# Blockwise-causal attention and an MLP mixer on one core: another order table for the whole run

## The chip, the core and the metric

The kernel runs on one core of a Trainium2 chip. The core has a matrix engine (TensorE: PE, with its weight loads shown apart as PEld), three engines that work on rows of data (VectorE: DVE, ScalarE: ACT, GpSimd: POOL) and a sync engine (SyncE: SP) that only issues transfers here. Each works through its own list of instructions in order, and waits on semaphores for the others. Transfers between HBM and the on-chip memory are issued by POOL, SP and ACT and carried out by 16 DMA engines.

The metric is the device time of one launch in microseconds (us). It is given as the median of several runs; one further execution, with the profiler on, gave the trace.

## The reference

Per batch (8) and head (8) a softmax attention over 576 positions with 64 columns a head, under a mask by blocks of 64; the heads are put side by side as `x` of 576 x 512. Then a mixer: across positions, then across columns, each with a residual.

```python
scores = scale * np.matmul(q, k.transpose(0, 1, 3, 2))     # q, k, v: [8, 8, 576, 64]
mask = (pos[:, None] // 64) >= (pos[None, :] // 64)
attn = softmax(np.where(mask, scores, -1e9))
x = np.matmul(attn, v).transpose(0, 2, 1, 3).reshape(8, 576, 512)
xt = x.transpose(0, 2, 1)
h = np.maximum(xt @ w_tok1, 0.0) @ w_tok2                  # 576 x 256, 256 x 576
u = x + h.transpose(0, 2, 1)
h2 = np.maximum(u @ w_ch1, 0.0) @ w_ch2                    # 512 x 1536, 1536 x 512
out = u + h2                                               # float32, [8, 576, 512]
```

## The kernel before

The kernel is written as a plan. Each piece of work is added by `P.add` with the engines that may do it, what it depends on and how many PSUM banks it takes: 1,492 operations in all, numbered in the order in which the code adds them. Nothing is issued while they are added. Then `P.placed()` walks a table of words, `ORDER` (lines 100 to 176), and issues the operations in its order:

```python
for word in ORDER.split():
    digits = word.rstrip("abcdefghstADPST")
    o, letters = self.ops[int(digits)], word[len(digits):]
    o.engine = self.ENGINE[letters[0]]
    ...
    for letter, (pools, note) in zip(letters[1:], o.take):
        note["pool"], note["slot"], note["home"] = pool_of[letter], self.SLOTS[letter][1], letter
```

The digits of a word are the operation's number. The first letter is its engine: T for TensorE, A for ScalarE, D for VectorE, P for GpSimd, S for SyncE. The letters behind it are the PSUM banks that it takes: a to d (`mm` in the profile), e to h (`late`), s and t (the two score banks of the opening, `sc`). The table therefore sets three things: the order of each engine's instructions, which of two engines does a piece where both may (evacuations of PSUM on ACT or DVE, the attention's tail copies on DVE or POOL, some stores on SP or ACT), and the banks. Waits follow from the data: an instruction waits for what wrote its operands, and for whoever read last what it overwrites.

The work of one batch passes these steps, with the lines that the profile names:

- Loads: q and k (`qk_sb`, L413 on POOL), transposed by DVE in blocks of 32 (L437); v in five pieces (`vals`, L463 on POOL). The weights come once: the token weights (L474), `w_ch1` in eight pieces of 192 KB (L497, `wc_sb`), `w_ch2` in three of 512 KB (L506, `wc_sb`).
- Scores: L562, four heads at a time, as tiles of 32 rows in four banks; ACT takes the exponentials into `e_sb` (L581 in the opening, L768 after it). A tail of 64 columns is copied into its own tile (L590) and its masked part cleared (L595), on DVE or POOL.
- Values: L612 and, for the last 64 positions, L665; DVE takes reciprocals (L632, L687) and scales into `x_sb` (L638, L693).
- Token mixing: L803, L807, then L836, L851 or L898, L929, L938; relus L789 (ACT) or L791 (DVE); DVE adds `u_sb` (L913). `u` is transposed by DMA on SP (L965, L975) or by TensorE (L985).
- Channel mixing up: L1026 plain, L1099 (`channel_up_half`) and L1226 (`channel_up_fast`) with products of sums and differences of blocks, for which `ws_sb` is made of the weights on DVE (L1057). Casts (L395 on ACT, L397 on DVE) and relus empty the banks.
- Channel mixing down: L1360, seven products of sums and differences of the relu's result (L1342) and of the weights, `wd_sb` (`weight_sums`, L1312, made by DVE once `w_ch2` is there). DVE folds the products with the residual into `o_sb` (L1406), which is stored (L1451; L1435 for the last 64 positions of all batches).

Where a product adds into a bank whose seed was written by another engine than TensorE, and which no matmul has opened, `cover` (L313) issues one more matmul into it first:

```python
def cover(bank):
    if P.bare(bank):
        nc.tensor.matmul(out=bank_of(bank), lhsT=ident, rhs=wc1_sb[:, 0, 0:512], start=True, stop=True)
```

`bare` looks at the pool that the table's bank letter stands for at that moment.

Of the kernel before, what the change touches and what calls it, by code (L numbers as in the profile page):

```python
# [27 lines left out]
class Plan:  # L28
# [72 lines left out]
    13S 16S 19S 22P 24P 5P 9D 2D 11D 8D 6D 3P 44Ta 12P 10P 4P 14D 30P 15D 17A 32P 1D 26P 18D 20A 28P 0A 45Tb 46Tc 47Td  # L101
    23D 25D 21D 7D 31D 174Tst 33D 175T 176A 177A 71Ta 61Tb 64Tc 182Ts 195A 196A 27D 81Td 183A 80Ta 201Tt 202A 60Tb 180Ts
    181A 29D 65Tc 197D 199Tt 76Td 178D 198D 36P 179D 200A 214Ts 215A 37P 35P 38P 34P 184Ta 188Tb 189T 190D 191D 207Tc
    208T 237Tt 238A 209D 210D 211Td 192Tb 216D 252P 254D 217D 193D 194D 220Ts 203Tc 204T 212D 213D 158P 205D 206D 185T
    155P 186D 221A 187D 218Tt 219A 233Ts 43P 156P 339Tb 239Tt 253D 340D 255P 257D 256D 234A 240A 42P 41P 39P 40P 337Td
    338A 222Tc 235D 236D 226Ta 227T 228D 223T 269Tbefg 271A 272A 249Th 224D 229D 225D 250D 251D 241Td 242T 243D 273A
    244D 157P 245Ta 246T 164P 247D 248D 348Tc 349T 350D 270A 281Tehfd 284A 230Tg 231D 282A 232D 343Ta 285A 261P 263D
    262D 258P 344D 276Tbcfg 277A 279A 159P 341Te 342A 280A 278A 283A 259D 260D 345Td 346T 347D 354Ta 355T 356D 313Tbfeg
    317A 316A 314A 315A 351Td 352T 353D 163P 387Tc 384Th 166P 301Taged 305A 390Tb 303A 302A 268P 165P 391T 274D 392D
    275D 388T 389D 304A 385T 306D 307D 308Tfdga 381Tb 264P 382T 408Te 409D 267P 312A 266P 265P 292Tc 295Ta 309A 318Tf  # L110
    386A 311A 296D 297D 289Th 290D 291D 160P 286Te 287D 288D 360Tg 366Ta 293D 310A 321Td 322D 323D 294D 319D 320D 400Th
    383A 416Tb 417A 161P 375Te 162P 376T 367T 368A 401A 421P 422D 423D 327Td 378Tc 372Tb 373T 374A 424P 328D 329D 404Tf
    405A 426D 377A 361T 427P 425D 428D 379T 380A 330Ta 362A 331D 332D 298Th 438Tdbfe 439A 430P 440A 324Ta 299D 432D 325D
    300D 369Tc 370T 326D 442A 429D 371D 450Tgdhb 441A 169P 363Ta 431D 364T 452A 333D 454A 451A 167P 357Te 358T 359A 365D
    393D 168P 482Tfcdb 485A 604P 484A 443P 453A 502Tg 436P 504Te 433P 503A 334D 335D 437P 435P 170D 486A 470Tadch 434P
    595P 505A 171D 444P 601P 483A 473A 445Tgbef 471A 172D 514Tc 448A 508Ta 472A 173D 515A 512Te 506Td 446A 509D 510Tc
    474A 513D 397Tgh 447A 475P 507D 449A 476P 394D 598P 477Tabef 398A 403Td 395D 480A 479A 511D 481A 493Te 396D 520Tb
    478A 490Tc 518Tf 521A 494D 407T 406D 519A 495D 597D 464Ta 596D 455Tb 461Tf 410D 458Te 399T 465D 491D 456D 457D 462D
    459D 466D 411T 463D 600D 402D 496Tb 522Ta 412D 516Tf 413T 523A 497D 599D 419S 517A 460D 762P 492D 499Tg 414D 759P
    467Ta 612Tdfec 498D 526D 415T 336D 615A 616A 614A 530Tcb 613A 487Te 500D 468D 469D 531Tf 533A 501D 617P 527D 545Tda  # L120
    532A 418D 618P 536T 611P 548A 524Tg 488D 489D 534Tf 537A 525D 610P 551T 528D 535A 624Thegc 605D 608P 552A 538T 606D
    628A 607P 540T 529D 627A 539D 678Td 626A 609P 603D 625A 549Tc 602D 679A 619Tgfeh 541D 550A 546Td 622A 760D 553T 623A
    763D 543T 620A 547D 676Te 621A 761D 544A 644Thgdf 542D 926P 677A 554D 555T 647A 764D 560Tbe 648A 556D 561Tc 929P
    563A 680Td 557D 765P 562A 684Tf 681D 645A 566T 558T 685D 646A 564Tc 567A 649D 559D 651Tdhgf 650P 565A 768P 638Tb
    653A 635Ta 772P 639D 568T 652A 640D 570T 636D 654A 637D 686Th 569D 655A 656Tbdga 571D 641Tf 660A 687D 629Tc 659A
    573T 642D 630D 689S 643D 632Ta 658A 631D 682Th 572D 657A 788Tgfdc 633D 634D 574A 673Tb 683D 790A 670Te 674D 789A
    664Ta 688S 675D 671D 579Tfh 672D 791A 665D 792A 666D 769D 783Tbgde 580A 667Tc 784A 661Ta 668D 581T 785A 669D 662D
    786A 663D 767D 787A 776Tbcgd 582D 842Ta 779A 766D 778A 575D 932P 840Te 780A 941P 770D 777A 583Tf 930D 773P 841A 576D
    843A 781P 820Tgcdb 939P 577D 585T 771P 821A 578D 824A 775P 584D 694Tae 850Tg 774P 690D 697A 587T 586D 822A 935P 691D
    823A 782P 692D 698Tb 851D 848Tc 588D 699A 700T 849D 695Tg 701A 704T 696D 702T 589T 705D 703D 693D 808Tdfca 931D 707T  # L130
    590D 810A 844Tg 812A 846Tb 845D 809A 793Tf 591T 708A 847D 811A 794D 795D 813P 815Tadge 592D 814P 805Tb 1024P 819A
    802Tc 594S 806D 818A 799Tf 807D 854S 803D 724Teh 817A 800D 709Tgb 801D 816A 727D 710Td 712A 725Tf 927D 711A 728Ta
    855S 928D 726A 715T 804D 796Td 729A 934D 730T 716A 713Tf 933D 731A 734T 420S 797D 798D 714A 732T 593S 735D 943Tcged
    733D 719T 945A 736D 717T 946A 720D 831Ta 944A 834Tg 718D 737T 947A 722T 835D 836D 738A 828Te 948P 832D 833D 950Tcfdg
    723A 829D 830D 837Th 721D 953A 852Ta 838D 952A 839D 857D 825Tb 951A 853D 876Tce 1036P 954A 877Td 858D 856S 879A 826D
    861Tfh 827D 1035P 878A 862Tg 859D 864D 891Tad 949P 863A 880Tb 940P 706D 894A 882T 739D 881A 942P 865Tg 897T 937D
    866A 938P 867T 936D 883A 884T 860D 1021P 868A 871T 885D 1030P 869T 898A 886T 872D 1027P 987Tcfba 870D 874T 887D
    1034P 990A 895Tg 988A 875D 889T 991A 1007Tb 740D 989A 896A 890D 955Tchaf 741D 892Te 959A 899T 1026D 956A 901T 893D
    958A 1009Tf 957A 1008D 902D 975Tcaeh 1010D 972Tb 978A 904T 900D 979A 960Tf 1025D 969Te 905A 743Tgh 961D 976A 973D
    1122P 974D 962D 977A 970D 971D 982Tdbcf 980D 744A 981D 1022D 966Ta 984A 963Te 1023D 745T 985A 967D 888D 1119P 986A  # L140
    964D 965D 983A 1037P 995Tb 968D 873A 998Tc 746D 1050Tfeda 1033P 996D 999D 992Tg 1000D 1054A 749T 993D 1053A 994D
    997D 1052A 1028D 1038Tcagd 1051A 1029D 1004Tb 1041A 1031D 1001Te 1125P 1040A 747Tf 1032D 1039A 1002D 1003D 1128P
    1005D 1006D 1082Tgace 1135P 748D 1017Tb 1084A 742D 751T 1083A 1018D 1086A 750D 1042A 1045Tageb 1085A 752D 1043P 753T
    1047A 1131P 1121D 757S 1049A 1120D 1044P 1048A 1077Tdcfg 754D 1064Tb 1080A 1124D 1061Te 755T 1046A 1065D 1062D 1063D
    1079A 1078A 1070Tfaec 1081A 756D 1067Td 1074A 1123D 1058Tg 1073A 1104Th 1066D 1059D 1071A 1060D 1130D 1072A 1055Tc
    1143Tbegf 1105A 1056D 1075P 1057D 1015Ta 1134P 1068D 1146A 1127D 1013Th 1145A 1069D 1102Tc 1129D 1147A 1076D 1144A
    1014D 1093Tg 1103A 1090Td 1016D 1136Tefbh 1126D 1020S 1099Tc 1137A 1094D 1114Ta 1091D 1092D 1140A 1100D 1087Te 1101D
    1139A 903D 1096Td 1088D 1112Th 1138A 1089D 758S 1108Tc 1095D 1115A 1141P 1113D 1106Tb 1132P 1175Tfeag 1097D 1142D
    1098D 1011Th 1133P 1107D 1179A 1336Td 1177A 1012D 1178A 1109D 1168Tgbeh 1176A 1110Ta 1116S 1171A 910Tcf 1170A 1111D
    1337A 1169A 1334Te 1117S 911D 906D 1148Tbadg 912T 907D 1150A 1019S 1172A 1151A 916T 1173P 913D 1152A 1174P 1149A  # L150
    908D 1118S 1180Tahdg 909D 1153Tc 1183A 914Tb 1154D 1184A 1155D 1181A 917D 1194Td 1182A 1335D 1159Tc 1191Tg 1195D
    1185Ta 1196D 1197Th 1160D 1192D 1165Te 1193D 920T 915D 1161D 1198D 1199D 1166D 1188Td 1167D 921D 1162Tg 1156Tc 1189D
    1249Teh 1190D 918T 1163D 1164D 1252A 1200D 1201D 922T 1186D 919D 1157D 1255T 1158D 924S 1279Tbd 1187D 923D 1280Tg
    1282A 1350Tc 1256A 1281A 1234Tea 1351A 1344Tf 1237A 1283Tc 1345D 1285T 1284A 1240T 1286A 1338Tg 1241A 1250Tf 1339D
    1253Tb 1251A 1287T 1202D 1254A 1348Te 1288D 1203D 1259T 1349A 1257T 1238Tc 1258D 1289T 1239A 1235Tg 1290D 1342Tf
    1236A 1244T 1291D 1343D 1356Te 1242T 1245D 1219Tbg 1243D 1360Tf 1260D 1220Tc 1361A 1357D 1262T 1222A 1292T 1364S
# [1404 lines left out]
```

## Time and profile before

| what | us |
|---|---|
| median of 3 runs | 287.9 |
| the three runs | 287.9, 285.44, 288.12 |
| the profiled execution | 286.21 |
| its span, first to last record | 284.4 |

The span is what the trace's times run over; the profiled execution's own time holds 1.8 us more, around it. The granted clock of TensorE was 0.997 of full speed in it. In the profile a line stands for engine, operation, output and input tile; "idle before" is the time that the engine stood still just before the group's instructions, with what ended that. TensorE's matmuls overlap one another, so the duration of one is longer than its distance to the next. Transfers are listed by the engine that issued them, with the time from issue to landing.

### The profile page before, as it was taken

To read this page: it belongs to the slowest core of one execution; us is meant where nothing else is said; L and a number is where in the kernel's file an instruction comes from. 1 tells how busy PE (TensorE), PEld (TensorE's weight loads), DVE (VectorE), ACT (ScalarE), POOL (GpSimd) and SP (SyncE) were. 2 spreads that over 40 slices of the span, in tenths; PEclk is the share of its full clock that TensorE was granted. 3 is DMA by queue.
4 is the path that set the end of the run, shared out by engine and by line. 5 is a ranking of instruction groups with operands and counts; after the bars stand their busy time and mean duration, and the time that the engine had idled before them with its cause. 6 is when DMAs were issued, how large, how long until landed. Compare 5 with 4: busy or idle time off the path is not lost.

```text
span 284.4 us, 9295 instructions
## 1 busy us (share of the span) xinstructions
PE 275.6 (97%) x3958; PEld 201.9 (71%) x3958; DVE 241.8 (85%) x520; ACT 178.3 (63%) x329; POOL 71.9 (25%) x123
## 2 busy tenths in 40 slices
PE   7799999999999999999999999999999999999994
PEld 2367565588776688986877658756789876568883
DVE  4678599999889898999998979859896997679983
ACT  3797969954998756887779866274533744651200
POOL 8977623701630451063232220000000000000000
PEclk9999999999999999999999999999999999999998
DMA  7999999955989792999699593201044501200157
GB/s 166 144 152 202 179 213 212 170 89 116 110 96 135 87 142 60 220 133 162 70 117 144 65 177 61 74 3 21 0 83 96 194 0 74 77 1 2 74 152 220
DMA packets 64890, 31.95 MB, mean 112 GB/s; under 512 B 53200, under 2 KB 55888, under 8 KB 64848
## 3 DMA queue, kind: packets, MB, share of 16 engines
q0 software_dynamic: 44896, 17.49, 53.9%
q1 hardware_dynamic: 19520, 13.21, 18.0%
q8 instruction: 31, 0.51, 0.7%
q10 hardware_dynamic: 432, 0.66, 0.7%
q14 instruction: 11, 0.09, 0.1%
HBM read 35.85 MB, written 9.44 MB: 159 GB/s over the span
## 4 chain that ended last, share of the span: by engine, by line
PE 78%; DMA 12%; DVE 4%; POOL 4%; issue 1%; POOLq 0%; DVEq 0%
PE late L1360 20%; DMA wc_sb<-in_moe_w_ch_dram 10%; PE mm L1360 9%; PE late L1226 8%; PE late L1099 7%; PE mm L1099 6%; PE mm L1226 5%; PE mm L562 4%; PE mm L612 3%; PE late L562 2%; PE late L898 2%; DMA qk_sb<-in_k_dram 2%; PE late L612 2%; PE mm L803 2%; PE late L803 2%; PE mm L898 1%
## 5 line engine op out<-in xcount | busy, mean ns | idle before, releaser
L768 ACT ACTIVATE e_sb<-late 128x512 bf16<-128x512 f32 x87 | 50.2, 612 | 15.0 <-PE late L562 6.6
L768 ACT ACTIVATE e_sb<-mm 128x512 bf16<-128x512 f32 x81 | 46.8, 611 | 5.9 <-PE late L562 3.3
L437 DVE STREAM_TRANSPOSE qk_sb<-qk_sb 128x288 int32<-128x288 int32 (+1 forms) x65 | 42.2, 694 | 2.7 <-DMA qk_sb<-in_q_dram 1.8
L463 POOL DMA_DIRECT2D vals<-in_v_dram x45 | 37.0, 834 | 7.1 <-PE mm L612 2.4
L1360 PEld LDWEIGHTS <-gT 128*128 128x128 bf16 x336 | 32.0, 98 | 6.0 <-issue 0.9
L1360 PEld LDWEIGHTS <-sums 128*128 128x128 bf16 x324 | 31.3, 98 | 5.3 <-issue 0.4
L562 PEld LDWEIGHTS <-qk_sb 32*64 32x64 bf16 (+1 forms) x1152 | 19.1, 103 | 16.3 <-issue 12.8
L562 PE MATMUL late<-qk_sb 32*64 32x448 bf16 (+7 forms) x530 | 28.1, 280 | 0.3
L562 PE MATMUL mm<-qk_sb 32*64 32x64 bf16 (+7 forms) x478 | 27.3, 280 | 0.1
L612 PEld LDWEIGHTS <-e_sb 128*128 128x128 bf16 x640 | 22.9, 97 | 4.1 <-issue 2.6
L395 ACT COPY mm<-late 128x512 f32<-128x512 f32 (+1 forms) x29 | 16.2, 568 | 13.1 <-PE late L1099 6.8
L1099 PEld LDWEIGHTS <-ws_sb 128*128 128x128 bf16 x192 | 18.2, 98 | 3.2 <-issue 0.9
L612 PE MATMUL mm<-vals,e_sb 128*128 128x65 bf16 x410 | 17.7, 193 | 0.7 <-DMA vals<-in_v_dram 0.7
L1360 PE MATMUL late<-wd_sb,sums 128*128 128x256 bf16 x150 | 18.3, 273 | 0.0
L638 DVE TENSOR_TENSOR x_sb<-mm,rinv 128x256 bf16<-128x256 f32 x41 | 16.9, 419 | 1.0
L1226 PEld LDWEIGHTS <-ws_sb 128*128 128x128 bf16 x120 | 11.7, 98 | 8.6 <-issue 0.2
L1099 PEld LDWEIGHTS <-wc_sb 128*128 128x128 bf16 x144 | 15.3, 114 | 1.6 <-issue 0.4
L1226 PE MATMUL late<-e_sb,ws_sb 128*128 128x512 bf16 (+1 forms) x72 | 16.2, 344 | 0.0
L789 ACT ACTIVATE gT<-mm 128x512 bf16<-128x512 f32 x21 | 12.8, 608 | 4.8 <-PE mm L1099 2.9
L413 POOL DMA_DIRECT2D qk_sb<-in_q_dram x14 | 7.7, 548 | 29.8 <-DVE x_sb L638 10.4
L1406 DVE TENSOR_TENSOR o_sb<-late,u_sb 128x512 f32<-128x512 f32 x20 | 13.6, 682 | 1.5 <-PE late L1360 1.4
L1360 PE MATMUL late<-wd_sb,gT 128*128 128x256 bf16 x120 | 14.8, 273 | 0.0
(200 smaller groups left out, 629.4 us busy)
## 6 DMA issues: line engine op xcount, KB each, us to landing
out_dram<-o_sb SPq DMA_DIRECT2D x19, 256.0 KB, 2.7
qk_sb<-in_k_dram POOLq DMA_DIRECT2D x14, 288.0 KB, 6.3
qk_sb<-in_q_dram POOLq DMA_DIRECT2D x14, 288.0 KB, 6.0
vals<-in_v_dram POOLq DMA_DIRECT2D x28, 128.0 KB, 5.3
out_dram<-o_sb SPq DMA_DIRECT2D x7, 512.0 KB, 3.8
wc_sb<-in_moe_w_ch_dram POOLq DMA_DIRECT2D x8, 192.0 KB, 7.1
wc_sb<-in_moe_w_ch_dram POOLq DMA_DIRECT2D x3, 512.0 KB, 12.6
vals<-in_v_dram POOLq DMA_DIRECT2D x15, 64.0 KB, 4.7
```

The source lines that it names most:

```text
L395: nc.scalar.copy(dst, src)
L437: nc.vector.transpose(dst[:, 0:S, :] .rearrange("p s e -> p (s e)") .bitcast(I32) .rearrange("p (a k) -> p k a", k=NB)[:, k0:k1], raw2.bit ...
L463: nc.gpsimd.dma_start(out=t[128 - p : 128, J, hs, 0:64], in_=src)
L562: nc.tensor.matmul(out=home(n)[lo : lo + rows, c : c + w], lhsT=bar[r, 0] if j is None else kT[i][r, 64 * j : 64 * j + rows, par], rhs=bar ...
L612: nc.tensor.matmul(out=u[:, I, 0:65], lhsT=e[:, h, c : c + 128], rhs=vt[:, J, head, 0:65], start=(J == 0), stop=(J == I),)
L638: nc.vector.tensor_tensor(out=xt[:, 0:4, 64 * head : 64 * head + 64], in0=u[:, :, 0:64], in1=ri[:, 0:4].to_broadcast([128, 4, 64]), op=MULT,)
L768: nc.scalar.activation(dst, bank_of(x), EXP, scale=scale)
L789: nc.scalar.activation(dst, src, RELU)
L1099: nc.tensor.matmul(out=bank_of(bank)[:, 256 * o_ : 256 * o_ + 256], lhsT=x(o_, m), rhs=y[:, :, m, :], start=opens, stop=m == 1, skip_group ...
L1226: nc.tensor.matmul(out=bank_of(bank)[:, 128 * c : 128 * (c + step)], lhsT=x(m), rhs=y[:, c : c + step, m, :], start=opens, stop=m == 1, sk ...
L1360: nc.tensor.matmul(out=bank_of(bank)[:, 256 * i : 256 * i + 256], lhsT=x[:, kk, 128 * i : 128 * i + 128], rhs=y[:, kk], start=first and i ...
L1406: nc.vector.tensor_tensor(out=dst, in0=src, in1=other, op=ADD)
```

## The change

The table `ORDER` is replaced by another; no other line differs. Both tables hold the same 1,492 operations. Two lines of the table's end, before and after:

```diff
-    1561D 1545D 1564T 1579D 1548S 1549A 1559D 1584T 1565D 1582T
-    1577D 1585D 1566T 1589A 1583D 1556T 1588A 1567D 1562T 1569S 1557D 1586T 1563D 1568S 1587D 1590S
+    1561D 1573D 1556T 1557D 1579D 1580T 1548S 1576T 1549A 1558Th 1553D 1582T 1577D 1581D 1583D 1588A 1564T 1559D 1565D
+    1584T 1585D 1589A 1562T 1563D 1568S 1566T 1567D 1569A 1586T 1587D 1590A
```

Counted over both tables, 39 evacuations go from ACT to DVE and 32 from DVE to ACT (25 and 17 of them after the point that lies at 180 us in the trace of before); 7 tail operations go from DVE to POOL and 5 from POOL to DVE; two stores go from SP to ACT. Two cover matmuls are no longer issued.

On POOL, at the place where the second batch's v and the channel weights are loaded (`vals` is v, `qk_sb` q or k, `wc_sb` a channel weight; `128x2048` is `w_ch2`), before:

```order
L497 DMA wc_sb<-in_moe_w_ch_dram 128x768 x3
L463 DMA vals<-in_v_dram 64x8x64
L497 DMA wc_sb<-in_moe_w_ch_dram 128x768
L463 DMA vals<-in_v_dram 128x8x64 x4
L497 DMA wc_sb<-in_moe_w_ch_dram 128x768 x3
L413 DMA qk_sb<-in_k_dram 128x1152
L413 DMA qk_sb<-in_q_dram 128x1152
L413 DMA qk_sb<-in_k_dram 128x1152
L413 DMA qk_sb<-in_q_dram 128x1152
L506 DMA wc_sb<-in_moe_w_ch_dram 128x2048 x3
```

And after, at the same place of POOL's list:

```order
L497 DMA wc_sb<-in_moe_w_ch_dram 128x768 x3
L413 DMA qk_sb<-in_k_dram 128x1152
L590 COPY vals<-e_sb 128x256
L595 MEMSET e_sb 64x4x64
L463 DMA vals<-in_v_dram 128x8x64 x3
L463 DMA vals<-in_v_dram 64x8x64
L463 DMA vals<-in_v_dram 128x8x64
L497 DMA wc_sb<-in_moe_w_ch_dram 128x768 x4
L413 DMA qk_sb<-in_q_dram 128x1152 x2
L413 DMA qk_sb<-in_k_dram 128x1152
L506 DMA wc_sb<-in_moe_w_ch_dram 128x2048 x3
```

A load of k and the second batch's first tail (copy and memset, which were on DVE) now stand ahead of all five loads of v and of four `w_ch1` pieces; the three `w_ch2` loads come last as they did.

On DVE, around the sums of weights for the down products (`wd_sb`) and the adds that give `u_sb`, before:

```order
L1342 TENSOR_TENSOR sums<-gT 128x1536
L1057 TENSOR_TENSOR ws_sb<-ws_sb,wc_sb 128x1536
L1057 TENSOR_TENSOR ws_sb<-wc_sb 128x1536
L1312 TENSOR_TENSOR wd_sb<-wc_sb 128x1536 x2
L1312 TENSOR_TENSOR wd_sb<-wc_sb,wd_sb 128x1536 x2
L913 TENSOR_TENSOR u_sb<-mm,x_sb 128x512
L913 TENSOR_TENSOR u_sb<-late,x_sb 128x512
L913 TENSOR_TENSOR u_sb<-mm,x_sb 128x512
L1342 TENSOR_TENSOR sums<-sums,gT 128x1536
L1342 TENSOR_TENSOR sums<-gT,sums 128x1536
```

And after:

```order
L1342 TENSOR_TENSOR sums<-gT 128x1536
L1057 TENSOR_TENSOR ws_sb<-wc_sb,ws_sb 128x1536
L791 TENSOR_SCALAR aT<-late 128x512
L1312 TENSOR_TENSOR wd_sb<-wc_sb 128x1536 x2
L1312 TENSOR_TENSOR wd_sb<-wc_sb,wd_sb 128x1536 x2
L437 STREAM_TRANSPOSE qk_sb<-qk_sb 128x9x32
L913 TENSOR_TENSOR u_sb<-mm,x_sb 128x512
L1342 TENSOR_TENSOR sums<-sums,gT 128x1536
L913 TENSOR_TENSOR u_sb<-late,x_sb 128x512
L913 TENSOR_TENSOR u_sb<-mm,x_sb 128x512
L913 TENSOR_TENSOR u_sb<-late,x_sb 128x512
L1342 TENSOR_TENSOR sums<-gT,sums 128x1536
```

A relu now stands ahead of the weight sums and a transpose between them and the first add, and the first sum of the relu's result is made between the first add and the second instead of after the third.

On SP the list of before ends with these stores:

```order
L1435 DMA out_dram<-o_sb 64x2x512 x3
L1451 DMA out_dram<-o_sb 128x512 x2
L1451 DMA out_dram<-o_sb 128x256
```

And on ACT the list of after ends with these, where before's ended with the first three alone, in the order 64x2x512, 128x256, 128x512:

```order
L1435 DMA out_dram<-o_sb 64x2x512
L1451 DMA out_dram<-o_sb 128x512
L1451 DMA out_dram<-o_sb 128x256
L1451 DMA out_dram<-o_sb 128x512
L1451 DMA out_dram<-o_sb 128x256
```

The last store of all, 128x256, and one of 128x512 ahead of it are now issued by ACT.

More of the change, by code (lines that the diff above doesn't have):

```diff
@@ L106 @@
[L106 to L110, printed above, removed]
@@ new lines @@
+    806D 928D 941P 704T 705D 724Tbh 819A 802Te 803D 804D 844Tg 807D 845D 706D 725Tc 940P 727A 730T 817A 850Te 851D 726A
+    709Tad 854S 937D 712A 828Tc 829D 728Tg 830D 710Te 707T 715T 729A 716A 734T 711A 927D 732T 731D 855S 708D 713Ta
+    943Tcbfe 733D 939P 714A 735D 831Tg 719T 717T 944A 934D 946A 945A 947A 834Tc 948P 737T 738A 720D 722T 835D 836D
+    950Tfbec 953A 718D 951A 832D 833D 723D 857D 954A 852Th 837Ta 952A 838D 861Teg 864A 876Tdf 877Tc 839D 858D 878A 879D
+    862Ta 865Tb 859D 860D 853D 1024P 863A 936D 867T 866A 868A 933D 880Tc 881A 871T 825Ta 1033P 872D 826D 736A 891Teh
```

135 lines of the change are left out of this document (67 added, 68 removed).

## The prediction

> **What bounds the kernel now.** I read the page's first part, then a table of busy time by stretches, then the list of TensorE's waits, then the chain.
>
> The page's first part gives each engine's busy time and its share of the span:
>
> ```profile
> PE 275.6 (97%) x3958; PEld 201.9 (71%) x3958; DVE 241.8 (85%) x520; ACT 178.3 (63%) x329; POOL 71.9 (25%) x123
> ```
>
> TensorE is the bound by its share, with VectorE not far behind. A share is a mean, so the table by stretches comes next. Its columns are the stretch, its length, busy us (and instructions) of PE, PEld, DVE, ACT and POOL, the granted clock, the DMA share and GB/s:
>
> ```profile
> 20.00:60.00 40.00, 38.62 (x716) 24.10 (x713) 34.78 (x79) 33.92 (x67) 20.07 (x34) 1.00 1.37 191
> 60.00:180.00 120.00, 119.91 (x2219) 92.51 (x2215) 111.47 (x263) 89.22 (x172) 34.91 (x56) 1.00 0.88 113
> 180.00:284.00 104.00, 100.45 (x774) 76.63 (x772) 83.48 (x144) 41.94 (x74) 0.00 (x0) 0.99 0.24 73
> 260.00:270.00 10.00, 10.00 (x94) 8.96 (x92) 10.00 (x18) 2.83 (x4) 0.00 (x0) 1.00 0.15 54
> 270.00:284.00 14.00, 10.45 (x96) 9.12 (x94) 8.85 (x20) 0.00 (x0) 0.00 (x0) 0.95 0.61 188
> ```
>
> From 60 us on TensorE has no hole until the end: 119.91 of 120, then full up to about 280.5. The clock is full. Two things stand out: in 260 to 270 VectorE is at 10.00 of 10 too, and in 20 to 60 TensorE misses 1.4 us. What it waits for, in order of total, with the number of waits and the longest:
>
> ```profile
> PE sc L562 <- DVE qk_sb L437: 1.5, 1, 1.5
> PE mm L367 <- DVE wd_sb L340: 1.2, 1, 1.2
> PE mm L612 <- DMA vals<-in_v_dram: 0.7, 2, 0.5
> PE sc L562 <- ACT e_sb L581: 0.4, 1, 0.4
> PE mm L803 <- DVE x_sb L638: 0.3, 1, 0.3
> PE mm L985 <- DVE u_sb L913: 0.2, 1, 0.2
> PE late L1360 <- ACT e_sb L768: 0.2, 1, 0.2
> ```
>
> That is 4.5 us in all. The first two and the fourth, 3.1 us, belong to the opening (first transposed q and k, the clock's warm-up matmuls, the first exponentials), whose order hardly changes. So at most 1.4 us of waits after it can be won. The rest is TensorE's own work, and the two tables issue the same tensor work, but for the two matmuls below.
>
> **The change part by part.** The sum is made against the profiled execution: 286.21 us, of which the span is 284.4.
>
> Two cover matmuls go. L313 issues one only where a bank that a later product adds to has not been written by a matmul; by the two tables' bank letters before has two such places and after none. In the profile they are these:
>
> ```profile
> L313 PE MATMUL mm<-wc_sb,ident x1: 379/379/379, 125.1 to 125.1; 128*128 128x512 bf16 x1
> L313 PE MATMUL late<-wc_sb,ident x1: 379/379/379, 179.6 to 179.6; 128*128 128x512 bf16 x1
> ...
> 46.70 0.38 PE L1026 MATMUL mm<-uT,wc_sb 128*128 128x512 bf16 x1
> 46.92 1.03 PE L1026 MATMUL late<-uT,wc_sb 128*128 128x512 bf16 x4
> ```
>
> The 379 ns overlap the next matmul; two of this shape start 46.92 − 46.70 = 0.22 us apart, and that is what one costs. Both lie in the full stretch: 2 × 0.22 = **−0.43 us**.
>
> Row modes. Scores run as 32-row tiles (L562), and a full-size product next to a score set takes longer than one that is not. In the chain (start, length, what, how many):
>
> ```profile
> 114.10 1.31 PE late L1099 x12
> 76.71 0.58 PE late L562 x23
> 77.29 1.42 PE mm L1099 x12
> ```
>
> The same 12 matmuls take 1.42 behind L562 and 1.31 elsewhere: 0.11 a switch. Counting neighbours in the tables, the borders of score sets go from 102 to 100, and those of the 64-wide end pieces (L665, L929) from 28 to 26. Two sets moved together save about 2 switches: **−0.2 us**, between 0 and −0.4.
>
> Evacuations between ACT and DVE. Counting engine letters, 39 evacuations (casts, relus) go from ACT to DVE and 32 back; after 180 us, 25 and 17. The same cast on each:
>
> ```profile
> L395 ACT COPY mm<-late 128x512 f32<-128x512 f32 (+1 forms) x29 | 16.2, 568 | 13.1 <-PE late L1099 6.8 <-PE late L1360 3.3 <-PE late L1226 2.6
> L397 DVE COPY mm<-late 128x512 f32<-128x512 f32 x5 | 3.5, 696 | 3.4 <-PE late L1099 1.7 <-PE late L1226 1.0 <-PE late L1360 0.7
> ```
>
> That is 0.13 us longer on DVE each. Beside TensorE's work it costs nothing: what hides it is that a bank comes free before TensorE asks for it, and no wait of TensorE's lies between 180 and 280 us. If that cover were gone everywhere, 25 × 0.13 = 3.3 us would show. In the last 20 us, where the 260 to 270 row has no idle VectorE, the tables put 5 more casts on DVE and take 2 away: 3 × 0.13 = **+0.4 us**; bounds 0 and 3.3.
>
> Tails ahead of loads. POOL's queue in 20 to 40 us gets the tail copy L590 and memset L595 of the second batch ahead of its five v loads; both wait for four exponentials, which in this run ended at 25.4 us. What stood there:
>
> ```profile
> 24.80 0.62 ACT L768 ACTIVATE e_sb<-mm 128x512 bf16<-128x512 f32 x1
> 29.09 0.88 POOL L463 DMA_DIRECT2D vals<-in_v_dram  x1 [0.98 <-DMA wc_sb<-in_moe_w_ch_dram]
> 37.42 0.53 POOL L506 DMA_DIRECT2D wc_sb<-in_moe_w_ch_dram  x1 [0.48 <-DMA wc_sb<-in_moe_w_ch_dram]
> DMA to landing us min/median/max: 6.1/7.7/8.6
> L590 POOL COPY vals<-e_sb x10: 402/403/410, 47.9 to 171.6; 128x256 bf16<-128x256 bf16 x10
> L595 POOL MEMSET e_sb<- x9: 307/307/307, 53.1 to 172.1; 64x256 bf16 x9
> 35.27 0.77 PE L612 MATMUL mm<-vals,e_sb 128*128 128x65 bf16 x20
> 35.87 1.07 PE L612 MATMUL late<-vals,e_sb 128*128 128x65 bf16 x30
> ```
>
> POOL passes the tail at 25.4 + 0.4 + 0.3 = 26.1 us. The fifth v load is then issued at 26.1 + 4 × 0.88 = 29.6 instead of 29.09, and lands 6.1 to 8.6 us later (the fourth row, for the v loads). The queue of transfers is full here (DMA share 1.37), and the same ten loads stand ahead of that place, so the data comes in the queue's turn rather than by its issue; TensorE uses it from 35.27 and 35.87 and waits for v in two places already. I take **+0.1 us**; if the 0.5 us of later issue went through, and the four wc loads behind too, up to +2; not under −0.5, the longer of the two waits that could vanish. The wc2 loads come later on POOL by about as much, and their last landing decides the next stage.
>
> The stage at 50 to 63 us. This is the stretch in which a transfer ends the chain:
>
> ```profile
> 37.42 14.09 DMA wc_sb<-in_moe_w_ch_dram
> ...
> 51.61 2.71 DVE wd_sb L1312 x3
> ...
> 55.21 1.88 DVE u_sb L913 x3
> ...
> 51.22 0.37 PE L562 MATMUL mm<-qk_sb 32*64 32x448 bf16 x1
> 51.71 0.84 PE L562 MATMUL late<-qk_sb 32*64 32x448 bf16 x2
> 52.20 0.21 PE L562 MATMUL late<-bar 32*64 32x64 bf16 x1
> ```
>
> The last wc2 load was issued 14.09 us before it landed, so a POOL that is 1 us later does not move it while the queue stays full. Behind it DVE makes wd_sb (L1312) and then the adds u_sb (L913), which free banks. After the change DVE has a relu (L791) and a transpose (L437) more ahead of the first add, by the cast above (0.696 for 128x512) about 0.7 each, an estimate; the relu lies in the time in which DVE waits for the landing, the transpose behind it. A sum (L1342) also stands between the first and the second. For: a product that needs the banks of those adds comes up to 0.7 us later. Against: the score set in the last three rows starts its pieces 0.49 us apart twice (51.22, 51.71, 52.20), about 1 us that the new place of the set may halve, and the 0.2 us wait of L985 for u_sb goes. I take **0**, between −1 and +1.
>
> Last stores. The last of all, 128x256, and one of 128x512 go from SP to ACT. By the table of issues (KB each, us to landing):
>
> ```profile
> out_dram<-o_sb ACTq DMA_DIRECT2D x1, 128.0 KB, 2.8
> out_dram<-o_sb SPq DMA_DIRECT2D x1, 128.0 KB, 2.0
> 280.49 0.42 DVE o_sb L1406
> ```
>
> The last fold ends at 280.9 and nothing covers what follows it, so 2.8 instead of 2.0 would show whole: +0.8. But the ACT stores were issued while the three of SP were moving, which lengthens them; I take **+0.5**, between 0 and +0.8. The Trainium skill, page "DMA: Bandwidth & Descriptors", section "Issuing engines are not separate DMA queues", has transfers of all issuing engines run on the same 16 DMA engines, with only the issue time saved by another issuer. By it this term would be 0 and the sum lower by 0.5; the rows differ by 0.8, but with unequal traffic beside them.
>
> Sum: −0.43 − 0.2 + 0.4 + 0.1 + 0 + 0.5 = +0.4 us, so 286.6 us by the profiled run. The profiled 286.21 lies 1.7 us under the median of the runs shown (287.9; the others 285.44 and 288.12). With it the four stand at 285.44, 286.21, 287.9 and 288.12, whose middle is 287.1, 0.9 above the profiled run. I add 0.6 of that, since the profile is a run like the others and half of the spread is chance: **287.2 us**.
>
> **The rivals.** First, slower: VectorE becomes the bound after 180 us. By the tables its work there rises by the 25 moved to it less the 17 moved away, 8 × 0.696 = 5.6 us, to 89 of 104, and in its full stretches (260 to 270: 10.00 of 10) there is no room. It decides where TensorE's lead over a bank's release falls under 0.13 us. For it: that row. Against: TensorE had no wait at all there, and 20 us of VectorE's 104 were idle. Price: all 3.3 us in place of the 0.4 in the sum, 286.6 + 2.9 = 289.5 by the profiled run, 290.1 as a median; with the last store at its upper bound, 290.4.
>
> Second, slower or level: POOL's late start on the v loads starves the transfer queue at 26 us, and the wc2 loads, last of that queue, come later with it. For: the chain there is DMA from 37.42 to 51.51. Against: 14.09 us of queueing in front. It decides if the queue runs dry before the late loads reach it, and costs +1 to +2 in place of 0.1: 287.5 to 288.5 by the profiled run, 288.1 to 289.1 as a median.
>
> Third, faster: the waits after the opening close. 1.4 us of TensorE waits in the list and the 1 us in the score set at 51 us, with −0.6 from covers and switches, and the last store at no cost: 286.21 − 1.4 − 1 − 0.6 = 283.2 at the least, 283.8 as a median; with half of the waits 284.4 and 285.0. For: the score set at 51 us has other work ahead of it now. Against: the same loads and the same wd_sb chain stand before the first product.
>
> **How the numbers follow.** Forecast as summed, within 1 us of 287.2: 0.45. First rival 0.20, second 0.15, third 0.20. What a measurement of this kernel can tell from no change is about 1%, 2.9 us on 287.9: faster means under 285.0, slower over 290.8. The third rival falls there in all but its weakest form; with what is left to it within 1%: 0.18 for faster. The first rival ends at 290.4 and passes 290.8 when the adds at 50 to 63 us also come late (+1), and the second does so only together with the first: 0.22 for slower. The rest, 0.60, is within 1%. The range reaches down to the middle of the third rival (283.8 to 285.0), 284.4, and up to the first rival with its store, 290.4, rounded to 290.5.
>
> **What would show it.** Right: no L313 rows; TensorE at 119.9 of 120 in 60 to 180; a list of waits with none on DVE after 180 us; a last store on ACT's queue that takes 2.0 to 2.8 us. The first rival shows as waits "PE <- DVE" of casts (L397) after 180 us; the second as L612 waiting for vals by more than 0.7 us or wc_sb landing after 52 us; the third as a missing hole at 51 to 55 us. Wrong it would be if TensorE's own steps changed length, which nothing in the tables says.

## The result, and the profile after

| | before | changed kernel |
|---|---|---|
| median of 20 runs each | 286.05 us | 286.19 us |
| lowest, highest | 284.94, 288.71 | 285.26, 288.1 |
| ratio, with its 95% interval | | 1.0001 (0.9981 to 1.002) |
| profiled execution, span | 286.21, 284.4 | 285.70, 283.9 |

No change that can be measured. (Here and below a median takes all runs; a ratio leaves out the few that lie over 1.5% above the kernel's fastest.) The 17 further runs of before brought its median from the 287.9 of the first three down to 286.05. Under that unchanged total a good deal moved, in both directions, and the traces show where.

The page of the changed kernel, first part, and then the six longest of TensorE's waits (total, number, longest):

```profile
PE 273.1 (96%) x3930; PEld 202.4 (71%) x3956; DVE 247.0 (87%) x525; ACT 176.2 (62%) x322; POOL 73.7 (26%) x125
...
PE sc L562 <- DVE qk_sb L437: 1.8, 1, 1.8
PE mm L367 <- DVE wd_sb L340: 1.2, 1, 1.2
PE sc L562 <- ACT e_sb L581: 0.9, 2, 0.6
PE late L562 <- DVE gT L1138: 0.7, 1, 0.7
PE mm L665 <- issue: 0.6, 1, 0.6
PE mm L612 <- DMA vals<-in_v_dram: 0.4, 1, 0.4
```

3,956 weight loads against 3,958: the two cover matmuls are gone. (26 matmul records are missing from this trace, those of L803, L851, L898 and one filler, so its PE total is not to be compared; a wait "for issue" in front of such a gap is not a wait either.) VectorE works 5.2 us more than before. The wait that before did not have is the fourth: a score set waits 0.7 us for an addition of VectorE, L1138, that joins two products. The chain of waits of the changed kernel shows what stands behind it (start, length, what):

```profile
70.13 0.41 POOL vals L590
70.55 0.05 issue
70.59 0.31 POOL e_sb L595
70.90 0.36 POOL vals L463
71.26 0.47 issue
71.73 7.24 DMA qk_sb<-in_k_dram
78.97 0.02 issue
78.99 0.07 DVE qk_sb L437
79.06 0.49 issue
79.55 1.24 DVE qk_sb L437 x2
80.78 0.53 DVE gT L1138
81.32 0.04 issue
81.36 0.22 PE late L562
```

And the same place in POOL's timeline, first of the changed kernel, then of before (start, length, instruction, in brackets the idle time ahead of it and what ended that):

```profile
64.87 0.54 POOL L413 DMA_DIRECT2D qk_sb<-in_q_dram  x1 [7.94 <-DVE rinv L632]
70.13 0.40 POOL L590 COPY vals<-e_sb 128x256 bf16<-128x256 bf16 x1 [4.72 <-ACT e_sb L768]
70.59 0.31 POOL L595 MEMSET e_sb<- 64x256 bf16 x1
70.85 0.89 POOL L463 DMA_DIRECT2D vals<-in_v_dram  x1
71.73 0.55 POOL L413 DMA_DIRECT2D qk_sb<-in_k_dram  x1
```

```profile
67.38 0.53 POOL L413 DMA_DIRECT2D qk_sb<-in_q_dram  x1 [10.42 <-DVE x_sb L638]
67.90 0.54 POOL L413 DMA_DIRECT2D qk_sb<-in_k_dram  x1
71.41 0.40 POOL L590 COPY vals<-e_sb 128x256 bf16<-128x256 bf16 x1 [2.98 <-ACT e_sb L768]
```

Read from the bottom: before issues a pair of q and k loads, then the tail copy, which has to wait for ScalarE. In the changed table the k load has slipped behind the tail copy and a v load. POOL works in order, and it stands 4.72 us in front of that copy, which waits for an exponential; so the k load is issued 6.9 us behind its q load (64.87 and 71.73) where before issues the two 0.5 us apart, and it lands at 78.97. VectorE, in order too, stands at the transposes of that k; behind them in its list is L1138, which frees the bank that the score set needs. So a wait of one engine passes through three queues.

At the other end of the span the changed kernel is quicker. The last fold, and the two stores of 128 KB with their time from issue to landing, of the changed kernel:

```profile
280.75 0.42 DVE o_sb L1406
...
out_dram<-o_sb ACTq DMA_DIRECT2D x2, 128.0 KB, 1.7
```

The fold ends at 281.17, the span at 283.9: 2.73 us, where before needed 284.4 − 280.91 = 3.49.

To see where time went between, I added up TensorE's steps (from the start of one instruction to the start of the next) in their order, each at the lower quartile of its kind in before, and noted by how much the trace is later than that sum. How much this lag grows, by stretches of TensorE's own work (us):

| work from..to | before | before again | changed | changed again | e11 | e1 | e9 | e10 |
|---|---|---|---|---|---|---|---|---|
| 0..20 | 5.10 | 5.53 | 4.94 | 7.57 | 4.87 | 5.08 | 6.63 | 6.60 |
| 20..60 | 8.24 | 7.85 | 7.41 | 7.41 | 7.41 | 8.17 | 7.81 | 7.45 |
| 60..100 | 2.73 | 2.39 | 3.93 | 4.16 | 4.39 | 2.66 | 2.66 | 2.66 |
| 100..250 | 11.90 | 11.90 | 11.95 | 11.93 | 11.94 | 11.95 | 11.94 | 11.94 |

All columns but "before" and "changed" are runs told of below. The last row is the striking one: 150 us of work with most of the moved evacuations in it differ by 0.05 us. The third has the new wait, about 1.5 us with what it holds up. The first two differ by chance as much as by order. How finely the kinds are drawn matters when two orders are compared: with other choices the changed kernel's last row came out up to 1.4 us above that of before, while runs of one order kept their differences to 0.1 us. So the 0.05 is an estimate, and a better one follows from e1.

### The profile page after: what moved, and what is told of

Same layout as the page of the kernel before. It is cut to its first block, busy times and chain, and to the rows that moved or that the text cites. A ratio compares the mean times of both kernels' runs of the same rounds, so it can differ in the third digit from the quotient of the medians.

```text
span 283.9 us, 9275 instructions
## 1 busy us (share of the span) xinstructions
PE 273.1 (96%) x3930; PEld 202.4 (71%) x3956; DVE 247.0 (87%) x525; ACT 176.2 (62%) x322; POOL 73.7 (26%) x125
## 4 chain that ended last, share of the span: by engine, by line
PE 83%; POOL 6%; DMA 5%; ACT 2%; issue 1%; DVE 1%; POOLq 0%
PE mm L1360 16%; PE late L1360 14%; PE late L1226 8%; PE late L1099 7%; PE mm L1226 5%; PE mm L1099 4%; PE late L562 4%; PE mm L562 3%; PE late L612 3%; PE mm L612 3%; DMA w_sb<-in_moe_w_tok_dram 3%; DMA qk_sb<-in_k_dram 3%; POOL vals L463 2%; ACT e_sb L768 2%; PE late L898 2%; PE mm L803 2%
## 5 line engine op out<-in xcount | busy, mean ns | idle before, releaser
L768 ACT ACTIVATE e_sb<-late 128x512 bf16<-128x512 f32 x83 | 48.3, 618 | 11.9 <-PE late L562 6.7
L768 ACT ACTIVATE e_sb<-mm 128x512 bf16<-128x512 f32 x85 | 49.0, 614 | 8.5 <-PE late L562 3.9
L562 PE MATMUL late<-qk_sb 32*64 32x64 bf16 (+7 forms) x494 | 27.9, 279 | 0.9 <-DVE gT L1138 0.7
L395 ACT COPY mm<-late 128x512 f32<-128x512 f32 x24 | 14.1, 592 | 10.3 <-PE late L1226 4.1
L590 POOL COPY vals<-e_sb 128x256 bf16<-128x256 bf16 x10 | 5.1, 506 | 51.6 <-ACT e_sb L768 51.6
L1226 PEld LDWEIGHTS <-ws_sb 128*128 128x128 bf16 x120 | 11.7, 98 | 8.1 <-issue 0.4
L789 ACT ACTIVATE gT<-late 128x512 bf16<-128x512 f32 x20 | 12.2, 619 | 8.0 <-PE late L1226 4.7
L1099 PEld LDWEIGHTS <-wc_sb 128*128 128x128 bf16 x144 | 15.1, 114 | 1.4 <-issue 0.4
L1226 PEld LDWEIGHTS <-wc_sb 128*128 128x128 bf16 x90 | 10.1, 113 | 5.7
L1360 PE MATMUL mm<-wd_sb,sums 128*128 128x256 bf16 x114 | 13.9, 273 | 0.0
L1226 PE MATMUL late<-e_sb,ws_sb 128*128 128x512 bf16 (+1 forms) x54 | 13.5, 356 | 0.0
L581 ACT ACTIVATE e_sb<-sc 128x1024 bf16<-128x1024 f32 (+2 forms) x14 | 11.6, 908 | 2.2 <-PE sc L562 2.2
## 6 DMA issues: line engine op xcount, KB each, us to landing
wc_sb<-in_moe_w_ch_dram POOLq DMA_DIRECT2D x3, 512.0 KB, 11.7
```

The costliest lines, as they stand in the source:

```text
L395: nc.scalar.copy(dst, src)
L562: nc.tensor.matmul(out=home(n)[lo : lo + rows, c : c + w], lhsT=bar[r, 0] if j is None else kT[i][r, 64 * j : 64 * j + rows, par], rhs=bar ...
L581: nc.scalar.activation(dst, sc[SC.index(note["pool"])][:, :, cols], EXP, scale=scale)
L768: nc.scalar.activation(dst, bank_of(x), EXP, scale=scale)
L789: nc.scalar.activation(dst, src, RELU)
L1099: nc.tensor.matmul(out=bank_of(bank)[:, 256 * o_ : 256 * o_ + 256], lhsT=x(o_, m), rhs=y[:, :, m, :], start=opens, stop=m == 1, skip_group ...
```

## The experiments

All but e6 are small edits of one of the two tables; the words are the operations' numbers with their engine and banks. "At full clock" below means the runs with a mean granted clock of 0.997 or more; "clock 0.990 or less" is counted apart, as the expectations set it.

**e1: the k load ahead of the tail copy.**

```diff
-    ... 762P 617P 618P 619Tfdbc 622A 543T 544A 607P 620A 623A 546Ta 606D 759P 764D
+    ... 762P 759P 617P 618P 619Tfdbc 622A 543T 544A 607P 620A 623A 546Ta 606D 764D
```

> The changed kernel with one word moved: the k load that POOL issues at 71.73 us stands ahead of the tail copy L590, which waits for ScalarE until 70.13. Theory (the order of POOL's queue makes the new wait of TensorE at 80 us): the load is issued at about 65 to 68 us and lands at least 3 us earlier than 78.97; VectorE's 1.73 us stand before its transposes falls under 0.5 and TensorE's 0.73 us wait for L1138 goes; the end comes 0.7 to 1.0 us earlier, 285.2 to 285.5. Rival (the load would land late anyway, held by the stores in flight, or the bank is late for another reason): landing after 77 us or a wait of the same size from another source; change under 0.3 us.

Measured: 285.54 us, ratio to before 0.9974 (0.9943 to 1.0006). From its trace, POOL's timeline, the landing of the two loads, and VectorE's timeline:

```profile
65.77 0.54 POOL L413 DMA_DIRECT2D qk_sb<-in_q_dram  x1 [7.94 <-DVE rinv L632]
66.30 0.54 POOL L413 DMA_DIRECT2D qk_sb<-in_k_dram  x1
71.04 0.40 POOL L590 COPY vals<-e_sb 128x256 bf16<-128x256 bf16 x1 [4.20 <-ACT e_sb L768]
...
DMA to landing us min/median/max: 4.9/5.3/5.8
...
76.92 2.86 DVE L437 STREAM_TRANSPOSE qk_sb<-qk_sb 128x288 int32<-128x288 int32 x5
79.90 0.69 DVE L1138 TENSOR_TENSOR gT<-late,half 128x512 bf16<-128x512 f32 x1
```

The k load is issued at 66.30 and is there by 72.1, nearly seven us earlier; the five transposes run without a stand and no wait of TensorE for L1138 is left. The lag over 60..100 falls from 3.93 and 4.16 to 2.66, about that of before. Both kernels give TensorE the same list, so its instructions can be set beside each other one by one: e1's gain comes whole between 79 and 82 us (1.27 us against the first profile of the changed kernel, 1.50 against its second), and from there to the end the distance stays within 0.03. The mechanism is shown, at 1.3 to 1.5 us rather than the 0.7 to 1.0 expected: the wait's row has the 0.7 us of one bank, and the rest can only lie in what stands around it, the set's other banks and the matmuls behind it. At full clock the median is 284.67 (5 runs), against 285.96 for before on the same chip (17 runs). Over all runs the interval still touches 1.

**e2: the last stores back on SP.**

```diff
-    ... 1567D 1569A 1586T 1587D 1590A
+    ... 1567D 1569S 1586T 1587D 1590S
```

> The changed kernel with the stores 1569 (128x512) and 1590 (128x256) back on SP. From the end of the last fold to the end of the span it took 2.73 us in the changed kernel and 3.49 before. Prediction's step (ACT is the slower issuer by 0.8): 0.5 to 0.8 us less than 2.73. Theory from the two traces (what counts is how many stores stand in the queue ahead of the last, not the issuer): 0.3 to 0.8 more than 2.73. Rival (the transfers share the engines whoever issues, and the difference is chance): within 0.2 of 2.73 plus what the issue itself takes.

Measured: 287.36 us, ratio 1.003 (0.9996 to 1.0064). Of its last fold and its 128 KB stores:

```profile
282.12 0.42 DVE o_sb L1406
...
out_dram<-o_sb ACTq DMA_DIRECT2D x1, 128.0 KB, 1.7
out_dram<-o_sb SPq DMA_DIRECT2D x1, 128.0 KB, 1.8
```

From the fold's end to the span's, 285.3 − 282.54 = 2.76: as long as with ACT (2.73). The issuer decides nothing, and my theory of a queue of stores falls with the prediction's. This agrees with the Trainium skill's "DMA: Bandwidth & Descriptors", section "Issuing engines are not separate DMA queues". Why before takes 0.75 us longer (3.59 in its second profile) is only half answered: its last store lands in 2.0 and 2.1 instead of 1.7 to 1.8, and about 0.5 us lie behind the landing, 1.43 and 1.46 us from there to the span's end against 0.93 and 0.96 in the changed kernel and e2. Most of that stands between two drain records of SP, 0.47 us apart in both profiles of before and 0.06 to 0.08 in the changed kernel and in e2. What SP does in that time was not tried. The 1.3 us that this run is slower than before are not in the tail: set beside the changed kernel's, its profile is already 1.37 us late at 82 us, ahead of anything in which the two kernels differ, and stays so; half of its runs were below full clock.

**e3: the late evacuations back on their old engines.** 42 words behind 180 us get before's letter, such as this one:

```diff
-    ... 1185Tf 1334Th 1335A 1186D
+    ... 1185Tf 1334Th 1335D 1186D
```

> The changed kernel with the 42 evacuations after 180 us that changed engine back on the engines of before (25 to ACT, 17 to DVE), order unchanged. Prediction's step (0.13 us each in the last stretch): -0.4 us. Prediction's first rival (VectorE is the bound there): -1 to -3 us. Theory now (TensorE waits nowhere there, VectorE's 90 of 104 us leave it its lead): within 0.3 us, and no wait of TensorE after 180 us in either.

Measured: 293.54 us, ratio 1.0233 (1.0186 to 1.0281); the one run at full clock took 291.67. All three expectations were wrong, the first two in sign too. The four longest of TensorE's waits after 180 us in e3, where the changed kernel has none at all:

```profile
PE mm L1226 <- DVE e_sb L1189: 2.0, 1, 2.0
PE mm L1360 <- DVE o_sb L1406: 0.9, 1, 0.9
PE mm L1099 <- ACT mm L395: 0.8, 1, 0.8
PE late L1226 <- ACT late L395: 0.7, 1, 0.7
```

VectorE has less to do there than in the changed kernel (85.4 us from 180 us to the end, against 89.9) and TensorE waits all the same, for ScalarE and for VectorE. The lag over 100..250 grows by 17.2 instead of 11.95.

**e4: 17 more late evacuations on DVE** (every third cast or relu that ACT still had there).

```diff
-    ... 1249Tcf 1240T 1252A 1241A 919D
+    ... 1249Tcf 1240T 1252D 1241A 919D
```

> The changed kernel with 17 more evacuations after 180 us on DVE instead of ACT, about 12 us more work for it there, 101 of 104. If TensorE's lead over the release of its banks is wide: under +0.5 us. If the changed kernel stands near the edge: +2 us or more, with waits of TensorE for L397 or L791. The 0.13 us per cast of the prediction alone would be +2.2.

Measured: 298.44 us, ratio 1.0391 (1.0345 to 1.0437); the one run at full clock took 296.17. The stretch from 180 us (after the two lengths: busy us and instructions of PE, PEld, DVE, ACT, POOL, then clock, DMA share, GB/s) and the longest wait in it:

```profile
180.00:294.00 114.00, 103.86 (x805) 77.16 (x807) 100.87 (x173) 31.03 (x49) 0.00 (x0) 1.00 0.24 71
...
PE late L1226 <- DVE mm L397: 2.4, 2, 1.6
```

The lag over 100..250 is 20.9: 8.9 us for 17 evacuations, 0.5 us each, four times the 0.13 by which DVE is slower at one. So it isn't the difference in duration that is paid. Two things can be: a place of some 0.7 us in a queue that is served in order, or a VectorE with no room left, which here is busy for 19.42 and 19.04 of the 20 us from 200 and from 220. e4 can't tell them apart; e3, where VectorE had less to do, speaks for the place in the queue.

**e8: before with the changed kernel's late engines.** The same 42 words, the other way round.

```diff
-    ... 1182A 1335D 1159Tc 1191Tg 1195D
+    ... 1182A 1335A 1159Tc 1191Tg 1195D
```

> The kernel before with the engines of the changed kernel for the 42 evacuations after 180 us that differ, its own order kept. If the engines of the changed kernel were simply better or worse: within 1 us of before, or the opposite of the cost of e3. Theory (order and engines were fitted to each other; each evacuation on the engine that is behind holds up a bank by its place in that engine's queue, about 0.7 us, not by the 0.13 us that it takes longer): +3 to +8 us, with waits of TensorE for casts after 180 us.

Measured: 290.47 us, ratio 1.0155 (1.0096 to 1.0213), and a lag of 15.9 over 100..250 for before's 11.90. TensorE, which waits nowhere after 180 us in before, does so six times here, 2.2 us in all, one of the longest:

```profile
PE late L1226 <- ACT e_sb L395: 0.5, 1, 0.5
```

So neither set of engines is the better one: with its own order each leaves TensorE no wait, with the other's it costs 4 to 5 us.

**e6: a cover matmul at each of the 58 seeded banks.**

```diff
-        if P.bare(bank):
+        if bank.get("seed", False):
```

> The changed kernel with a cover matmul (L313) at all 58 seeded banks instead of none. The prediction's price (0.22 us each, whole on the bound): +12.8 us, 298 to 300. Rival (TensorE's lead or its overlap hides part): +6 or less.

One run: 302.75 us, with a mean granted clock of 0.966; the half clock lies in the opening (0.50 from 9 to 21 us, 0.89 over 21 to 60). Between the first cover at 61 us and the end the lag behind the changed kernel grows from 6.1 to 16.9, so 10.8 us for 58: 0.19 each. At 80 us it falls by 0.9, for there e6 no longer has the wait for L1138: covers issued before it only fill that wait. Without this it is 11.7 us, 0.20 each. The price of 0.22 stands, a little high; nothing hides a cover but a wait that is there anyway.

**a1 and b1: both kernels once more**, as they are.

> The changed kernel itself once more, on the chip of this call, as the base for the others. Theory (the new wait at 80 us is in every run; the opening's waits for q, k and v are chance and differ by up to 2 us between profiles of one order): TensorE's 0.7 us wait for L1138 again, the opening's waits of another size than 1.8 (qk_sb) and 0.4 (vals); time within 0.3% of before. Rival (the first profile was the usual one): the opening's waits within 0.2 us of the first profile's.

> The kernel before itself, for a second profile of it. Theory (the opening's waits are chance): its waits before 25 us differ by 0.3 us or more from 1.5 (qk_sb) and 0.7 (vals), and the 1 us gap in the score set at 51 us is there again since the order makes it. From the end of the last fold to the span's end it took 3.49 us; if the 0.5 us beyond the others is chance, about 3.0 here.

The changed kernel: 287.71 us, ratio 1.0055 (1.002 to 1.009), where the first measurement had 1.0001; before: one run of 285.94. The wait for L1138 is there again, 0.7 us. The clock is new. The stretches of the opening, first of a1, then of the changed kernel's first profile (the granted clock is the third number from the right):

```profile
5.00:9.00 4.00, 1.90 (x30) 0.83 (x29) 2.40 (x5) 0.93 (x4) 4.00 (x7) 0.99 1.04 149
9.00:19.00 10.00, 9.27 (x103) 3.77 (x103) 3.48 (x10) 6.21 (x9) 9.38 (x15) 0.50 1.50 155
```

```profile
5.00:9.00 4.00, 1.56 (x31) 0.66 (x30) 2.97 (x5) 1.33 (x4) 4.00 (x8) 1.00 1.05 156
9.00:19.00 10.00, 9.57 (x215) 5.96 (x216) 6.04 (x24) 8.98 (x11) 9.38 (x15) 1.00 1.51 153
```

TensorE does little from 5 to 9 us in both; in one the clock is then at half for 10 us, which costs the 2.6 us of the lag table's first row. Six of a1's twelve runs had a mean clock of 0.990 or less, with times of 288.59 to 289.9; the other six, at 0.998 or more, 286.04 to 286.82. In before's 46 runs beside e1 to e4 (23) and beside a1 (23) none was so low. The changed kernel's first measurement had one of 20, but the runs that share its opening order had 17 of 36 (e1 5 of 12, e2 4 of 12, e3 3 of 6, e4 5 of 6). The Trainium skill's "TensorE: Matmul & The Clock Gate", section "What's actually happening", has the clock halved after about 3.4 us of idling, in windows that run free of the kernel; the half clock, and that it comes in some runs only, agree with that.

The opening's waits differ between profiles of one order as expected: for the first q and k 1.5 and 1.0 us in before, 1.8 and 1.9 in the changed kernel, 0.6 in e1 and 2.7 in e2; for v 0.7 and 1.6, 0.4 and none. From the last fold to the end before takes 3.59 after its 3.49; e8 and e12, told of next and below, keep before's end and take 3.5 and 3.4, and all runs with the changed kernel's end take 2.7 to 2.9. So that difference is no chance.

**e9: e1, and a k load of the opening behind four v loads.**

```diff
-    ... 339Ta 252P 43P 41P 42P 39P 217D ...
+    ... 339Ta 43P 41P 42P 39P 252P 217D ...
```

> The changed kernel with two loads moved in POOL's list: the k load of e1, and in the opening the second batch's first k load (issued 13.1 us) behind the last four v loads of the first batch. Theory: the v loads land about 1.4 us earlier (288 KB less ahead of them), TensorE's 0.4 to 1.0 us wait of L612 for vals at 21 us goes, the k load lands 1.4 us later than 19.2 to 20.4, still ahead of its use; with e1's 1.3 to 1.6 us the time comes to 284.0 to 285.0 where before is 286.06. Rival (the v loads wait elsewhere, or TensorE then waits for the transposes of that k load): no further gain on e1, a wait of L562 for qk_sb at 25 to 30 us in place of that for vals.

Measured: 286.48 us, ratio 1.0003 (0.997 to 1.0037); at full clock 284.72 (3 runs), what e1 has alone. The rival was right. The wait for vals is gone and another of 2.1 us stands in its place. Its row names a reciprocal, L632; VectorE's timeline shows what held that up, the transposes of the moved load:

```profile
PE late L562 <- DVE rinv L632: 2.1, 1, 2.1
...
21.48 1.80 DVE L437 STREAM_TRANSPOSE qk_sb<-qk_sb 128x288 int32<-128x288 int32 x3 [2.42 <-DMA qk_sb<-in_k_dram]
```

**e12: before with a hole in the opening; e11 and e10: the changed kernel's hole filled.** Where the fillers (L374) stand, of before, of the changed kernel, of a1 and of e11, by TensorE's timeline:

```profile
5.87 0.92 PE L374 MATMUL mm<-wd_sb 128*128 128x512 bf16 x3
8.97 0.82 PE L374 MATMUL mm<-wd_sb 128*128 128x512 bf16 x3
```

```profile
5.36 0.81 PE L374 MATMUL mm<-wd_sb 128*128 128x512 bf16 x3
9.63 0.81 PE L374 MATMUL mm<-wd_sb 128*128 128x512 bf16 x3 [0.16 <-issue]
```

```profile
5.70 0.81 PE L374 MATMUL mm<-wd_sb 128*128 128x512 bf16 x3
10.47 1.49 PE L374 MATMUL mm<-wd_sb 128*128 128x512 bf16 x3 [0.33 <-issue]
```

```profile
5.87 1.25 PE L374 MATMUL mm<-wd_sb 128*128 128x512 bf16 x3
7.93 1.04 PE L374 MATMUL mm<-wd_sb 128*128 128x512 bf16 x4
```

From the end of one group to the start of the next: 2.2 us in before, 3.5 and 4.0 in the changed kernel, 0.8 in e11. (Two short score steps lie in each of the first three.) It is 3.6 in e12, and only 2.3 in e1, which has the changed kernel's opening: how late the first q and k come counts too. The edits of e12 and e11; e10 has e11's and e1's:

```diff
-    ... 174Tst 33D 175T 176A 177A 71Ta 61Tb 64Tc 182Ts 195A 196A 27D 81Td 183A 80Ta 201Tt
+    ... 174Tst 33D 175T 176A 177A 182Ts 195A 196A 27D 81Td 183A 80Ta 71Ta 61Tb 64Tc 201Tt
...
-    ... 174Tst 176A 175T 177A 81Ta 76Tb 195A 197D 196A 33D 198D 60Tc 61Td 201Ts
+    ... 174Tst 81Ta 76Tb 60Tc 61Td 176A 175T 177A 195A 197D 196A 33D 198D 201Ts
```

> The kernel before with three of its fillers moved from behind the first score set to behind the next, so that TensorE has the same 3.4 us or more with little work as the changed kernel (6.8 to 10.2 us). Theory: runs at a mean clock of 0.990 or less, 0 of 46 of before so far, in a third or more of 12; median up by 0.5 to 2 us. Rival (something else of the changed order drops the clock): none, median within 0.3 of before.

> The changed kernel with the four filler matmuls moved and nothing else. Same theory: at most 1 of 12 runs at a mean clock of 0.990 or less, median 286.0 to 286.5, ratio to before within 0.2% of 1; TensorE's 0.7 us wait for L1138 at 80 us still there. Rival (chance of the chip): half of the runs at 0.990 or less and a median of 287 or more, as in the changed kernel again (287.71).

> The changed kernel with the k load of e1 moved and, in the opening, four of the clock's filler matmuls (L374) between the two halves of the first score set, where TensorE stood from about 6.5 to 10 us with two score steps of 0.1 us in it. Theory (the granted clock falls to half when TensorE does too little for some 3 us in the opening; the changed order leaves 3.4 to 4.4 us there, before 2.2 to 3): runs with a mean granted clock of 0.990 or less, 5 and 6 of 12 in e1 and the changed kernel again, come in at most 1 of 12; median 284.6 to 285.2 with before at 286.0, ratio 0.995 to 0.997. Rival (the clock falls by chance of the chip): as often as in e1, median 285.5 or more.

| | median | ratio to before (95%) | runs with clock 0.990 or less | median at full clock |
|---|---|---|---|---|
| before, on the same chip | 286.23 | | 5 of 29 | 286.0 |
| e12 | 289.48 | 1.0066 (1.002 to 1.0111) | 7 of 12 | 286.32 |
| e11 | 286.37 | 1.0002 (0.9962 to 1.0041) | 1 of 12 | 285.91 |
| e10 | 285.79 | 0.9996 (0.9959 to 1.0032) | 3 of 12 | 284.85 |

e12 says that the hole is enough to make the drop frequent: the same operations as before, three fillers later, and 7 of 12 runs lose clock where 5 of 29 did. That filling it keeps the clock is not shown. e11 has one of 12, where the changed kernel had 6 of 12, but on another chip; e10, with the hole filled too, has 3 of 12; and counted below 0.997 there are 6 and 8 of 12 in e11 and e10, against 8 of 29 in before. The traces say why: the half clock does not come in the hole alone. In e10's profile it lies from 21.4 to 24.8 us, behind a wait of 1.4 us for the token weights, and in e9's from 24.4 to 27.8, behind the 2.1 us shown above. So the hole makes the drop more frequent and is not its only place. e10 is not shown to be faster than before over all its runs.

## Why the prediction came out as it did

The sum, +0.4 us or 286.6 by the profiled run, lay 0.4 above the median measured (286.19) and 0.9 above the changed kernel's own profiled run (285.70). What failed in the forecast as it stood is the step from the sum to a median: "I add 0.6 of that". The three runs shown had a median of 287.9, and 17 more show that this lay high in a spread of 284.94 to 288.71; the profiled 286.21 was the better witness of the 286.05 that all 20 give. With that step the forecast said 287.2, 0.7 below the median shown, and so a gain that no term of the sum contained; measured was a change of +0.1, which is none.

Inside the sum three terms were mis-sized. That they nearly cancel, and the sum comes out close, is luck:

- Last stores: +0.5 predicted, −0.75 measured (3.49 and 3.59 against 2.73 and, in a1, 2.69). I read 2.8 and 2.0 us of two rows as the two issuers'; e2 shows that they weren't (1.8 from SP, 1.7 from ACT). The Trainium skill's rule that stood beside it, 0 for the issuer, was the better one; the −0.75 comes from elsewhere, and from where stays open.
- Tails ahead of loads: +0.1 predicted for 25 us, and there it holds (no wait of TensorE for v at 35 us, and the last `w_ch2` piece lands at 50.9 us, not later than the 51.5 of before). But the same pattern at 70 us, one k load behind a tail copy, costs 1.3 to 1.5 us, as e1 shows. I had priced one place that the tables' difference showed and not looked for the others. The second rival's "+1 to +2" had the price and POOL's late issue right, but not the rest: there no v load and no `w_ch2` load held anything up; one k load, 45 us later, stood behind a waiting POOL.
- Late casts: +0.4 predicted, about 0 found (+0.05 by the lag over 100..250, and the balance below leaves no more). The reason given was wrong. "No wait of TensorE's" was taken for a wide margin, and the margin is next to none: e3, e4 and e8 turn 17 to 42 of these choices and lose 4 to 9 us. The first rival's condition ("under 0.13 us") was thus nearly met, and its price of 0.13 an evacuation was four times too low, by e4; that it did not come is the fit of this order to these engines, which neither table's counts show.

What held: the covers (−0.43 predicted, 2 × 0.20 = −0.4 by e6). The row modes' −0.2 was not tried by itself. The stage at 50 to 63 us was put at 0 ± 1; over 20..60 the lag is 7.41 in both profiles of the changed kernel and 8.24 and 7.85 in before, and e1, which differs from the changed kernel in nothing before 64 us, had 8.17. So a gain of up to 0.6 is possible there, and not shown.

With these the balance closes: −0.4 (covers), −0.75 (tail), 0 to −0.6 (20..60), +1.5 (60..100), +0.05: +0.4 to −0.2, and at full clock the changed kernel's median is 286.02 in its first measurement and 286.21 in a1, before's 285.91 to 286.0 on three chips. e1 tests it without the lag table: it lacks the new wait, and at full clock lies 1.3 us under before on the same chip; covers and tail alone make −1.15. For the late casts, the row modes and 20..60 together about −0.15 is left, less than the spread of the runs. The third rival was half right too: two small waits did close (0.2 us for `u_sb`, 0.2 for an exponential), but most of the gain came from the tail and the covers, and the new wait took it.

"The clock is full" was read from one profile. It is a matter of chance in this opening, and the prediction had no term for it.

## What to carry to other kernels

Where engines work in order, compare every load's place in its issuer's list with the nearest instruction that waits for another engine, over the whole run: one load behind one waiting copy cost more here than 71 evacuations on other engines, whose order had been fitted to them. That an engine never waits does not tell how near it is to waiting; turn a few choices and see. And take a stretch in which TensorE does little as a price in itself, paid in some runs only: the clock of many runs, not of one profile, tells whether the order provokes it. Before a sum is carried over to a median, measure the median: three runs were too few for a change of 0.3%.

## What the runs showed of the hardware

In a1 a half clock began at 8.9 us, 2.4 us after a group of fillers had ended, and stayed for 10.2 us although TensorE was called busy for 9.27 of the 10 us from 9 to 19; it took 2.6 us of the run. The mean clocks of whole runs come in steps (1.0, 0.994, 0.988, 0.982); 0.006 of 284 us is 1.7 us, half of 3.4, as if half clock were granted in pieces of 3.4 us. The clock records of the traces show such pieces: inside the span half clock lasts 3.41 us in e9, e10 and e12, 10.24 in a1 and 20.48 in e6, which is 1, 3 and 6 of them. That agrees with the free-running windows of the Trainium skill's "TensorE: Matmul & The Clock Gate", section "What's actually happening". Its idle window is more than was needed here, as follows.

Counted back in pieces of 3.41 us from these starts (in traces without one, from the half clock behind the last instruction), the piece just before a half clock had TensorE busy for 0.41 of it in a1, 0.45 in e6, 0.46 in e12, 0.40 in e9 and 0.59 in e10. Pieces that kept the clock are as low as 0.46 (e3), so no sharp limit comes out of these traces; but none of the five was idle. In the opening the least busy piece of the first profiles has 0.47 in the changed kernel and 0.55 in before.
